# Three layers on one core: the first layer's last six chunks go by seven products in pairs of blocks

## The chip, the cores and the metric

The kernel runs on one core of a Trainium2 chip. The core has five engines with queues of their own: TensorE (PE, matrix products into PSUM, which has eight banks here), VectorE (DVE), ScalarE (ACT), GpSimd (POOL, no access to PSUM) and SyncE (SP, which here only issues DMAs). The metric is the device time of one execution in microseconds (us).

## The reference

Attention with a threshold, and behind it two layers of two products each, on 2304 tokens of width 512:

```python
scores = scale * np.matmul(q, k.transpose(0, 1, 3, 2))          # 4 x 8 heads, 576 x 576, depth 64
thresh = np.max(scores, axis=-1, keepdims=True) - tau
scores = np.where(scores >= thresh, scores, -1000000000.0)
...                                                             # softmax, times v, heads side by side
h = x @ w_in                       # first layer, 512 -> 2048
r = np.maximum(h, 0.0)
g = s * (r * r) + b                # s and b are one number each
x = g @ w_out                      # 2048 -> 512
h = x @ w_in2                      # second layer
g = np.maximum(h, 0.0) + alpha * np.minimum(h, 0.0)
out = g @ w_out2
```

## The kernel before

Everything is float32. A product is made of three matmuls in a faster format: each operand is split into a high and a low part (`mm3`, L512 to L515: low x high, high x low, high x high). So each operand costs a copy on ACT, which makes the high part, and a subtraction on DVE or POOL, which makes the low part. The weights come as 64-bit numbers and are turned into float32 by shifts and masks on DVE (`numbers`).

The program is a list of tasks. Each has an engine or a choice of engines, a duration, buffers and a rank. A planner (`Plan.run`) plays them in time and gives each free engine the ready task of lowest rank; the order that comes out is each engine's order. Two tables, `MOVED_RANKS` and `MOVED_TASKS`, shift single ranks. Transfers have an assumed time in the planner too.

Four stages follow each other on TensorE:

- A: attention, 16 pairs of heads. Transposes bring q and k into place; for the pairs 4 to 15 the split q is copied on by DMA, from `hq` into `q` or `qo`, two copies for each head (L735), before the head's score products (L775) can start. In between, the first layer on the first 1536 tokens, in six blocks of 256, with the first 10 of 16 chunks of 128 columns of w_in. Each chunk passes relu, square, scale and shift (`square`, L548 to L566); the partial sums go to DRAM (`ya`).
- B: the rest of the first layer, in blocks of 384 tokens. The last two blocks take all 16 chunks, the first four blocks the chunks 10 to 15. A chunk is four products of w_in with a quarter of x each (`hidden`), `square_b` (L568 to L586), and four products with w_out.
- C: the second layer's first product. Two blocks are taken together, and a two by two product of quarters is made by seven products and additions (`seven`, and the loop from L1176): operands are sums of quarters, and results come together by ACT copies out of a bank (L1205), DVE additions (L1209) and more matmuls on top of the same bank. 24 such units.
- D: the second layer's second product, also by seven, in nine blocks of 128 rows from each of two blocks. The last additions (L1300, L1304) and stores (L1312) end the program.

Of the kernel before, what the change touches and what calls it, by code (L numbers as in the profile page):

```python
# [17 lines left out]
P = 128  # L18
BIG = 3.0e38
REBIAS = 2.0 ** -112  # L20
NA = 10
# [12 lines left out]
COLD = 5.5  # L34
# [4 lines left out]
BUSY = 180  # L39
# [23 lines left out]
}  # L63
MOVED_TASKS = {
# [74 lines left out]


class Task:
    __slots__ = ("ways", "engine", "fn", "bufs", "needs", "next", "tail", "port")


class Plan:
# [107 lines left out]
def tile_kernel(ctx: ExitStack, tc: tile.TileContext, q, k, v, tau, w1i, w1o, s_in, b_in, w2i, w2o, alpha, out):  # L253
# [732 lines left out]
    with tc.manual_schedule():  # L986
# [24 lines left out]
        for u in range(NA // 2):  # L1011
            u1i[u] = Unit(w1i, "1i", u, W1I[0] + W1I[1] * u, early=True)
# [342 lines left out]
```

## Time and profile before

| | |
|---|---|
| median of 3 runs | 1106.6 us (1106.44 to 1107.65) |
| the profiled execution's own time | 1106.05 us |
| its span, first to last instruction | 1104.2 us |
| granted TensorE clock | 1.00 throughout |
| TensorE busy (matmul) | 1083.9 us, 98% of the span |
| VectorE busy | 912.9 us, 83% |
| ScalarE busy | 762.2 us, 69% |
| GpSimd busy | 347.9 us, 32% |

Busy time is the union of an engine's instructions. Matmuls overlap, so a matmul's own duration (0.33 us for 384 columns) is longer than its share of the engine; the distance from one start to the next is the share. An idle time of an engine is put down to what ended last before it went on.

### The profile page before, as it was taken

The numbers are of one execution on the slowest core, as the hardware profiler recorded it, in microseconds if no ns is written. First come the engines' busy times: TensorE is split into PE (matmuls) and PEld (weight loads), VectorE is DVE, ScalarE is ACT, GpSimd is POOL, SyncE is SP. The second block draws the span as 40 slices with busy tenths as digits, with TensorE's granted clock in tenths as the row PEclk, the third lists the DMA queues.
The fourth block names the chain that finished last, engine by engine and source line by source line (L and its number), as shares of the span: only waits on it lengthen the run. The fifth ranks groups of instructions, "written<-read, shape, count | busy, mean of one in ns | idle before, by whom it ended". The sixth has DMA issues, their size and how long they took to land.

```text
span 1104.2 us, 22123 instructions
## 1 busy us (share of the span) xinstructions
PE 1083.9 (98%) x7552; PEld 1050.5 (95%) x7552; DVE 912.9 (83%) x2043; ACT 762.2 (69%) x1752; POOL 347.9 (32%) x473
## 2 busy tenths in 40 slices
PE   9899999999999999999999999999999999999998
PEld 8677899999999999999999999999999999999998
DVE  5798888888978988666887789889867999999882
ACT  5787877877877877565464467478777987565551
POOL 1576754654736547231000011112100331212111
PEclk9999999999999999999999999999999999999999
DMA  6654454446444553106366554857535475564531
GB/s 125 172 164 130 108 125 129 110 119 156 110 118 99 133 144 81 47 13 202 116 200 191 176 178 150 284 194 236 170 115 165 166 216 163 148 172 131 143 99 39
DMA packets 185265, 158.36 MB, mean 143 GB/s; under 512 B 72000, under 2 KB 162112, under 8 KB 185152
## 3 DMA queue, kind: packets, MB, share of 16 engines
q1 hardware_dynamic: 181424, 154.49, 48.9%
q10 hardware_dynamic: 3728, 2.46, 0.8%
q8 instruction: 59, 0.97, 0.4%
q14 instruction: 54, 0.44, 0.1%
HBM read 91.10 MB, written 44.56 MB: 123 GB/s over the span
## 4 chain that ended last, share of the span: by engine, by line
PE 82%; DVE 7%; ACT 4%; DMA 3%; issue 2%; SPq 1%; POOL 1%; DVEq 0%; ACTq 0%; POOLq 0%
PE bank L513 13%; PE bank L515 13%; PE bank L514 13%; PE bank_b L514 7%; PE bank_b L515 7%; PE bank_b L513 7%; PE sc L775 7%; PE bank L884 7%; PE bank L909 5%; PE bank L913 1%; DMA q<-hq 1%; PE bank L692 1%; DMA qo<-hq 1%; DMA nat<-in_k_dram 1%; DVE wa L491 1%
## 5 line engine op out<-in xcount | busy, mean ns | idle before, releaser
L789 DVE SCALAR_TENSOR_TENSOR e<-sc,mx,e 128x576 f32<-128x576 f32 x144 | 116.1, 812 | 16.7 <-ACT e L787 14.9
L909 PE MATMUL bank<-eyes,e 128*128 128x128 f32 (+1 forms) x640 | 118.7, 274 | 2.5 <-ACT gf L919 1.4
L783 DVE TENSOR_REDUCE mx<-sc 128x1 f32<-128x576 f32 x144 | 107.4, 751 | 14.8 <-PE sc L775 14.1
L513 PE MATMUL bank<-gt,wa 128*128 128x256 f32 (+1 forms) x372 | 116.0, 312 | 0.4 <-ACT rest L551 0.4
L787 ACT ACTIVATE e<-sc,mx 128x576 f32<-128x576 f32 x144 | 106.1, 744 | 13.3 <-DVE mx L783 12.7
L514 PE MATMUL bank<-gt,wa 128*128 128x256 f32 (+1 forms) x372 | 111.8, 301 | 0.1
L515 PE MATMUL bank<-gt,wa 128*128 128x256 f32 (+1 forms) x372 | 111.8, 301 | 0.0
L909 PEld LDWEIGHTS bank<-eyes,e 128*128 128x128 f32 (+1 forms) x640 | 79.7, 139 | 15.2 <-ACT gf L919 2.8
L513 PE MATMUL bank<-xt,wa 128*128 128x256 f32 (+1 forms) x261 | 82.0, 314 | 0.3 <-ACT rest L551 0.3
L785 POOL TENSOR_SCALAR mx<-mx,tau_s 128x1 f32<-128x1 f32 x144 | 47.2, 330 | 94.4 <-DVE mx L783 89.7
L515 PE MATMUL bank<-xt,wa 128*128 128x256 f32 (+1 forms) x261 | 74.7, 286 | 0.0
L514 PE MATMUL bank<-xt,wa 128*128 128x256 f32 (+1 forms) x261 | 74.7, 286 | 0.0
L513 PEld LDWEIGHTS bank<-gt,wa 128*128 128x128 f32 x372 | 70.3, 189 | 1.2 <-ACT rest L551 0.6
L514 PEld LDWEIGHTS bank<-gt,wa 128*128 128x128 f32 x372 | 70.4, 189 | 0.3 <-POOL gt L564 0.3
L515 PEld LDWEIGHTS bank<-gt,wa 128*128 128x128 f32 x372 | 70.3, 189 | 0.0
L775 PE MATMUL sc<-k,q 128*128 128x288 f32 x256 | 61.8, 366 | 2.9 <-DMA q<-hq 1.5
L884 PE MATMUL bank<-gl,vt 128*128 128x256 f32 (+1 forms) x192 | 63.5, 332 | 0.2 <-DVE gl L944 0.2
L884 PE MATMUL bank<-gh,vt 128*128 128x256 f32 (+1 forms) x192 | 57.7, 302 | 0.0
L944 DVE TENSOR_TENSOR gl<-bank,gh 128x256 fp32r<-128x256 f32 (+1 forms) x96 | 43.2, 451 | 15.9 <-ACT gh L942 15.5
L574 ACT ACTIVATE gt<-rest,b_b,s_b 128x384 fp32r<-128x384 f32 x56 | 39.4, 707 | 23.9 <-DVE rest L572 23.2
L954 POOL TENSOR_TENSOR gr<-gf,gh 64x256 fp32r<-64x256 f32 (+1 forms) x48 | 39.4, 822 | 42.1 <-DVE gl L952 37.1
L775 PEld LDWEIGHTS sc<-k,q 128*128 128x128 f32 x256 | 41.5, 190 | 10.4 <-DVE e L789 3.3
(723 smaller groups left out, 4033.9 us busy)
## 6 DMA issues: line engine op xcount, KB each, us to landing
stg<-in_moe_w_in_dram SPq DMA_DIRECT2D x32, 512.0 KB, 4.1
stg<-in_moe_w_out_dram SPq DMA_DIRECT2D x32, 512.0 KB, 4.2
qo<-hq SPq DMA_DIRECT2D x30, 256.0 KB, 4.5
gf<-rest SPq DMA_DIRECT2D x35, 192.0 KB, 1.9
rest<-gf SPq DMA_DIRECT2D x42, 128.0 KB, 3.0
q<-hq SPq DMA_DIRECT2D x18, 256.0 KB, 4.4
xr<-xs SPq DMA_DIRECT2D x6, 768.0 KB, 4.5
yf<-yb SPq DMA_DIRECT2D x24, 192.0 KB, 2.9
```

The costliest lines, as they stand in the source:

```text
L513: nc.tensor.matmul(o, lhsT=wl, rhs=mh, start=first, stop=False, skip_group_check=on_top)
L514: nc.tensor.matmul(o, lhsT=wh, rhs=ml, start=False, stop=False, skip_group_check=on_top)
L515: nc.tensor.matmul(o, lhsT=wh, rhs=mh, start=False, stop=last, skip_group_check=on_top)
L574: t = add("ACT", act(n, 2, True), lambda: nc.scalar.activation(g.t[:, 0, :n], r.t[:, :n], AF.Identity, bias=b_b, scale=s_b), (r,), (g,), r ...
L775: nc.tensor.matmul(sp.t[:, x, :HS], lhsT=o[0][:, c], rhs=o[1][:, x * HS:(x + 1) * HS], start=n == 0, stop=n == len(passes) - 1)
L783: add("DVE", dve(S), lambda sp=sp, mx=mx: nc.vector.tensor_reduce(mx.t[:, 0:1], sp.t[:, :, :HS], op=ALU.max, axis=AX.XY, negate=True), (sp ...
L785: t2 = add("POOL", 0.26, lambda mx=mx: nc.gpsimd.tensor_scalar(mx.t[:, 1:2], mx.t[:, 0:1], -1.0, tau_s, op0=ALU.mult, op1=ALU.subtract), ( ...
L787: add("ACT", act(S, 1), lambda sp=sp, mx=mx, e=e: nc.scalar.activation(halves(e.t), sp.t[:, :, :HS], AF.Exp, bias=mx.t[:, 0:1]), (sp, mx), ...
L789: add("DVE", dve(S) + 0.065, lambda sp=sp, mx=mx, e=e, col=col, sums=sums: nc.vector.scalar_tensor_tensor(halves(e.t), sp.t[:, :, :HS], mx ...
L884: nc.tensor.matmul(o.t[:, :n], lhsT=w.rearrange("p a b -> p (a b)"), rhs=m.t[:, :n], start=c == first and x == 0, stop=c == last and x == ...
L909: nc.tensor.transpose(gt.t[:rows, m:m + P], es[i].t[:, keys], ident)
L944: add("DVE", dve(n), lambda hi=hi, lo=lo, gt=gt: nc.vector.tensor_tensor(lo.t[:, :n], gt.t[:, :n], f32(hi.t[:, :n]), op=ALU.subtract), (gt ...
```

## The change

1. First layer, B. The last two blocks now go through the chunks 0 to 9 alone, as before with `hidden`, and write partial sums to `ya`. After that three pairs of blocks (0,1), (2,3), (4,5) take the chunks 10 to 15 by seven products: three units for each pair, each of two chunks and two blocks. The weights of these six chunks are made into the seven operands once, x into seven operands for each pair and half. The product with w_out stays as it was, chunk by chunk. At the end the partial sums from `ya` are added.
2. Scale and shift leave the chunks. With r the relu, (s r r + b) @ w_out is s (r r @ w_out) + b times the sums of w_out's columns. The sums of columns are built by adding up the w_out tiles (`total`) and four matmuls of one column; ACT applies s and the shift when an output leaves its bank, and one DVE instruction adds s times the partial sum.
3. The second layer's weights are split later: unit 0 from the end of B's first part on, units 1 to 3 in B's last pair, the rest behind B.
4. In the last block of D each of the seven products has a bank of its own.
5. q, k and v are loaded with one DMA for two heads, not one for each. In the first four pairs the two heads' q buffers count apart.
6. The planner's transfer times are new (a start, a time in a common queue, a tail), and both tables of shifts are new, about as long as before.

```diff
 MOVED_RANKS = {
-    10: -53.2, 50: -14.5, 50.1: -0.3, 75: -27.5, 80.1: -30.1, 85: 42.9, 170.1: -6.8, 180: 36.5, 185: 15.7, 195: -32.8, 200: -38.5, 200.1:
...
+    50: -4.5, 50.1: 9.1, 75: -11.4, 95: 37.2, 110: 10.1, 115: 26.1, 140.1: 30.3, 145: -2.5, 150: -9.3, 170: -6.5, 201: 54.1, 205: 16.6, 207:
...
-    def hwdge(fn, reads=(), writes=(), rank=None, kb=128, after=()):
-        return add("SP", 0.6, fn, reads, writes, after, rank, tail=Plan.LAND + kb / 180.0)
...
+    def moved(kb, run):
+        return kb * 64.0 / run * (0.0075 + 0.000051 * run)
...
+    def hwdge(fn, reads=(), writes=(), rank=None, kb=128, run=1536, tail=1.3, after=()):
+        return add("SP", 0.655, fn, reads, writes, after, rank, tail=tail, moved=moved(kb, run))
...
+            if not inner:
+                add([("POOL", pool2(DM), rank), ("DVE", dve(DM), rank + 0.5 * LATER)], 0, lambda e: on(e).tensor_tensor(
+                    total, total, n32.t, op=ALU.add), (n32, of_total), (of_total,), after=(t,), port=True)
...
-            if e == "DVE":
-                nc.vector.scalar_tensor_tensor(x, x, s_b, x, op0=ALU.mult, op1=ALU.mult)
-                nc.vector.tensor_scalar(x, x, b_b, None, op0=ALU.add)
-            else:
-                nc.gpsimd.tensor_tensor(x, x, x, op=ALU.mult)
-                nc.gpsimd.tensor_scalar(x, x, s_b, b_b, op0=ALU.mult, op1=ALU.add)
...
+        add([("POOL", pool2(n), SOON), ("DVE", dve(n), others)], 0, lambda e: on(e).tensor_tensor(
+            r.t[:, :n], r.t[:, :n], r.t[:, :n], op=ALU.mult), (r,), (r,), port=True)
...
-                loads[nm] = [load(nm, 128, lambda e, t=t, src=src, h=h: e.dma_start(
-                    t.t[:, 0:NQ, h, :], src[b, h0 + h, 0:NQ * P, :].rearrange("(p c) d -> p c d", c=NQ)), t) for h in range(2)]
+                loads[nm] = [load(nm, 256, lambda e, t=t, src=src: e.dma_start(
+                    t.t[:, 0:NQ], src[b, h0:h0 + 2, 0:NQ * P, :].rearrange("h (p c) d -> p c h d", c=NQ)), t)]
...
+        def sums_of_columns():
+            for d in range(NC):
+                nc.tensor.matmul(pb.t[:, d:d + 1], lhsT=total[:, d * P:(d + 1) * P], rhs=ones, start=True, stop=True)
...
-        order = sorted(range(len(blocks_b)), key=lambda j: (blocks_b[j][0] < NJA * TA, j))
-        for i, j in enumerate(order):
-            c0, n = blocks_b[j]
-            f0 = NA if c0 < NJA * TA else 0
...
-            stream(range(f0, NF), first, second)
+        pairs = [(0, 1), (2, 3), (4, 5)]
+        for i, j in enumerate(pairs[-1]):
...
+            for f in range(NA + LAG):
...
+        for i, js in enumerate(pairs):
...
+            xq = quarters(xs, lambda b, c, cs=cs: of_xs(cs[b], n), cs, bx_s, xc)
...
+            for c in range(2):
+                ops, sums = seven(xq[c], False, n, bx_s, None, xb_s, None, SOON + 1e-3, ("DVE",), IN_PLACE)
...
+            def product(k, h, start, after, w, xo=xo):
+                def go():
+                    for c in range(2):
+                        mm3(h.t[:, :n], w[k].t[:, 0, c * P:(c + 1) * P], w[k].t[:, 1, c * P:(c + 1) * P],
+                            xo[c][k].t[:, 0], xo[c][k].t[:, 1], start and c == 0, c == 1, True)
...
+            for u in range(NB):
...
+                product(1, ha, True, (), w)
+                p1, t = copy(ha)
...
+                product(2, hb, True, (), w)
+                plus(hb, p1)
+                squared(p1, 0, fa)
+                product(5, hc, True, (), w)
+                p5, t5 = copy(hc)
+                product(6, ha, False, t, w)
+                pu, t = copy(ha)
...
+                    add("ACT", act(n, 2), lambda y=y, t=t, d=d: nc.scalar.activation(
+                        t.t, y.t[:, :n], AF.Identity, bias=shift[:, d:d + 1], scale=s_b), (y, of_shift), (t,), rank=SOON)
...
+                    add("DVE", dve(n) + 0.065, lambda p=p, t=t: nc.vector.scalar_tensor_tensor(
+                        t.t, p.t, s_b, t.t, op0=ALU.mult, op1=ALU.add), (p, t), (t,), x, SOON + 0.5 * (i == len(pairs) - 1), port=True)
...
-                acc = [Buf(moe_s) for _ in range(4)]
+                each = 1 if (i, it) == (len(pairs) - 1, TB // P - 1) else 2
+                acc = [Buf(moe_s) for _ in range(-(-7 // each))]
```

The order of the instructions moves almost everywhere in A. Three places are shown.

SP in A, at the copies from `hq` for two scores, in a row before (`stg` holds x of the first layer, `xs` and `ya` are in DRAM; the score that comes next reads `q_133`):

```order
L731 DMA k_134<-hk_136 64x576 x2
L658 DMA nat_131<-in_v_dram 128x4x64 x2
L526 DMA stg_99<-xs 128x4x256
L1036 DMA ya<-rest 128x2x256
L735 DMA qo_1284<-hq 64x2x512
L735 DMA q_133<-hq 64x2x512 x2
L735 DMA qo_1284<-hq 64x2x512
L665 DMA nat_131<-in_v_dram 64x2x64
```

And SP in A now, at such copies (the score that comes next reads `qo_1275`):

```order
L730 DMA ko_1277<-hk_139 64x576 x2
L730 DMA k_137<-hk_139 64x576
L655 DMA nat_134<-in_v_dram 128x8x64
L662 DMA nat_134<-in_v_dram 64x2x64
L734 DMA qo_1275<-hq 64x2x512 x2
L734 DMA q_136<-hq 64x2x512 x2
L665 DMA nat_134<-in_v_dram 64x2x64
L730 DMA k_137<-hk_139 64x576
```

Before, one copy for the later score stands ahead of the two that are needed first; now the two that are needed first stand together and ahead. The load of v is one DMA of 128x8x64 where it was two of 128x4x64.

TensorE in B before, one chunk's product with w_in (`xb` are the four quarters of x, `wb` a w_in tile, 12 matmuls into one bank):

```order
L513 MATMUL bank_105<-xb_5998,wb_5977 128x384
L514 MATMUL bank_105<-xb_5998,wb_5977 128x384
L515 MATMUL bank_105<-xb_5998,wb_5977 128x384
L513 MATMUL bank_105<-xb_5999,wb_5977 128x384
L514 MATMUL bank_105<-xb_5999,wb_5977 128x384
L515 MATMUL bank_105<-xb_5999,wb_5977 128x384
L513 MATMUL bank_105<-xb_6000,wb_5977 128x384
L514 MATMUL bank_105<-xb_6000,wb_5977 128x384
L515 MATMUL bank_105<-xb_6000,wb_5977 128x384
```

And TensorE in B now, one of the seven products (`bank_111`) between products with w_out (`bank_b_5785`, whose operands lie in `wa`):

```order
L527 MATMUL bank_b_5785<-wa_95,wa_91 128x384
L528 MATMUL bank_b_5785<-wa_95,wa_91 128x384
L529 MATMUL bank_b_5785<-wa_95,wa_91 128x384
L527 MATMUL bank_111<-xb_5776,wb 128x384
L528 MATMUL bank_111<-xb_5776,wb 128x384
L529 MATMUL bank_111<-xb_5776,wb 128x384
L527 MATMUL bank_111<-xt,wb 128x384
L528 MATMUL bank_111<-xt,wb 128x384
L529 MATMUL bank_111<-xt,wb 128x384
```

A product is now six matmuls over two operands of x (there are two halves of the rows), and seven of them stand for what were 16 products of three matmuls, two chunks and two blocks.

TensorE at the program's end before, products 3 and 7 of the last block, both into `bank2`:

```order
L513 MATMUL bank2_107<-gt_104,xt_103 128x256
L514 MATMUL bank2_107<-gt_104,xt_103 128x256
L515 MATMUL bank2_107<-gt_104,xt_103 128x256
L513 MATMUL bank2_107<-wa1_89,wb2_5979 128x256
L514 MATMUL bank2_107<-wa1_89,wb2_5979 128x256
L515 MATMUL bank2_107<-wa1_89,wb2_5979 128x256
```

And now, the same two products:

```order
L527 MATMUL bank0_108<-wa9_100,gt_107 128x256
L528 MATMUL bank0_108<-wa9_100,gt_107 128x256
L529 MATMUL bank0_108<-wa9_100,gt_107 128x256
L527 MATMUL bank1_109<-wa8_99,gt_107 128x256
L528 MATMUL bank1_109<-wa8_99,gt_107 128x256
L529 MATMUL bank1_109<-wa8_99,gt_107 128x256
```

The additions that read product 3 no longer wait for the matmuls of product 7.

## Rows read from the trace of the kernel before

**Rows 1.** The page's head: busy time, share of the span and instructions of each engine.

```profile
span 1104.2 us, 22123 instructions
...
PE 1083.9 (98%) x7552; PEld 1050.5 (95%) x7552; DVE 912.9 (83%) x2043; ACT 762.2 (69%) x1752; POOL 347.9 (32%) x473
```

**Rows 2.** Four stages: span, then busy time (and count) of PE, PEld, DVE, ACT, POOL.

```profile
0.00:505.60 505.60, 492.05 (x3688) 461.58 (x3689) 413.49 (x933) 381.13 (x855) 264.96 (x381) 1.00 0.47 119
505.60:739.00 233.40, 233.34 (x1344) 232.48 (x1343) 191.55 (x382) 138.08 (x264) 21.07 (x22) 1.00 0.57 181
739.00:918.00 179.00, 177.20 (x1018) 175.29 (x1016) 153.84 (x303) 145.21 (x359) 35.21 (x39) 1.00 0.56 182
918.00:1104.20 186.20, 181.36 (x1506) 181.14 (x1506) 154.00 (x428) 97.82 (x276) 26.69 (x31) 1.00 0.45 126
```

**Rows 3.** Starts and durations of 384-column matmuls, eleven in a row.

```profile
739.06 0.33 PE L514 MATMUL bank_b<-xb,wa 128*128 128x384 f32 x1
...
740.79 0.33 PE L515 MATMUL bank<-gt,wb 128*128 128x384 f32 x1
```

**Rows 4.** The critical chain: small fp32 matmuls (two records each), start and duration.

```profile
11.56 1.12 PE bank L860 x10
```

**Rows 5.** TensorE's waits up to 505 us: total, times, longest.

```profile
PE sc L775 <- DMA q<-hq: 3.2, 2, 1.7
...
PE sc L775 <- DMA qo<-hq: 1.3, 2, 1.0
```

**Rows 6.** The critical chain at two of those waits, on either copy.

```profile
263.74 6.05 DMA q<-hq
...
384.86 7.13 DMA q<-hq
```

**Rows 7.** VectorE's groups of instructions: busy, mean ns, idle before.

```profile
L572 DVE TENSOR_TENSOR rest<-bank,rest 128x384 f32<-128x384 f32 x30 | 16.5, 553 | 8.7 <-ACT rest L571 8.5
...
L581 DVE TENSOR_SCALAR rest<-rest,s_b,b_b 128x384 f32<-128x384 f32 x25 | 11.9, 478 | 7.4 <-ACT gt L574 7.3
...
L491 DVE TENSOR_TENSOR wa<-sm,wa 128x256 fp32r<-128x256 f32 x35 | 15.8, 464 | 0.1
...
L1172 DVE SCALAR_TENSOR_TENSOR yb<-yb,nal_b,yat 128x384 f32<-128x384 f32 x2 | 2.2, 1076 | 0.0
...
L1172 DVE SCALAR_TENSOR_TENSOR rest<-rest,nal_b,of 128x384 f32<-128x384 f32 x5 | 3.1, 614 | 0.3 <-ACT of L1171 0.3
```

**Rows 8.** VectorE's groups up to 505 us.

```profile
L556 DVE SCALAR_TENSOR_TENSOR rest<-rest,s_b 128x512 f32<-128x512 f32 x14 | 11.3, 805 | 5.0 <-ACT rest L551 5.0
...
L564 DVE TENSOR_TENSOR gt<-rest,gt 128x512 fp32r<-128x512 f32 x12 | 9.8, 815 | 1.3 <-ACT gt L563 1.2
...
L557 DVE TENSOR_SCALAR rest<-rest,b_b 128x512 f32<-128x512 f32 x14 | 7.7, 551 | 0.5
```

**Rows 9.** Busy time where the second layer's first product ends, as in Rows 2.

```profile
880.00:900.00 20.00, 20.00 (x118) 19.96 (x117) 19.84 (x46) 19.61 (x55) 7.10 (x9) 1.00 0.77 240
900.00:920.00 20.00, 18.28 (x108) 17.35 (x107) 19.47 (x41) 14.85 (x40) 6.88 (x8) 1.00 0.58 182
```

**Rows 10.** TensorE's waits from 739 us on.

```profile
PE bank L513 <- DVE xr L1209: 0.8, 1, 0.8
PE bank_b L513 <- ACT yb L1205: 0.7, 1, 0.7
```

**Rows 11.** The last instructions: start, duration.

```profile
1098.79 0.42 DVE L1300 TENSOR_TENSOR n<-bank,xr 128x256 f32<-128x256 f32 x1 [1.02 <-PE bank L515]
...
1099.13 0.42 DVE L1300 TENSOR_TENSOR rest<-bank,xr 128x256 f32<-128x256 f32 x1
1099.19 0.28 PE L515 MATMUL bank_b<-xb,xt 128*128 128x256 f32 x1
...
1099.79 0.42 DVE L1300 TENSOR_TENSOR yat<-bank_b,rest 128x256 f32<-128x256 f32 x1
...
1100.58 0.71 ACTq L1312 DMA_DIRECT2D out_dram<-rest  x1
```

More of the change, by code (lines that the diff above doesn't have):

```diff
@@ L141 @@
 class Task:
-    __slots__ = ("ways", "engine", "fn", "bufs", "needs", "next", "tail", "port")
+    __slots__ = ("ways", "engine", "fn", "bufs", "needs", "next", "tail", "port", "moved")
 class Plan:
@@ L223, in run @@
                         at(now + us, "free", e)
-                        at(now + us + t.tail, "end", t)
+                        if t.moved:
+                            moving = max(moving, now + Plan.ARRIVE) + t.moved
+                            at(moving + t.tail, "end", t)
+                        else:
+                            at(now + us + t.tail, "end", t)
                         break
@@ L360, in tile_kernel @@
     x_s, xb_s, xr_s = Slots(cut(xt, TA)), Slots(), Slots()
[L361 removed]
+    g_s, gb0_s = Slots(cut(gt, 2 * TA)), Slots()
     def pieces(t):
@@ L401, in mult @@
                 on(e).tensor_scalar(n32.t, f32(word(1)), REBIAS, None, op0=ALU.mult)
-        hwdge(load, (), (raw, *also), rank, 512, after)
+        hwdge(load, (), (raw, *also), rank, 512, 1024 if inner else 4096, 1.3, after)
         add([("DVE", 0.34, rank), ("ACT", act(DM, 0, True), rank)], 0, mult, (raw,), (n32,), port=True)
@@ L711, in scaled @@
                                     nc.scalar.activation(q32[p][:, c], tr.t[:, of], AF.Copy, scale=sc_h[h])
-                            add([("DVE", dve(n) + 0.065, ready), ("ACT", act(n, 1), ready)], 0, scaled, (tr,), (hl,))
+                            x = (add([("DVE", dve(n) + 0.065, ready), ("ACT", act(n, 1), ready)], 0, scaled, (tr,), (qt if tail else qs[h],), x),)
                         continue
@@ L1078, in tile_kernel @@
         of_w = []
-        def stream(fs, first, second):
-            gs = {}
-            for i in range(len(fs) + LAG):
-                if i < len(fs):
-                    gs[fs[i]] = first(fs[i])
-                if i >= LAG:
-                    second(fs[i - LAG], gs.pop(fs[i - LAG]))
-        RB = 2 * LATER
-        full = [last]
-        order = sorted(range(len(blocks_b)), key=lambda j: (blocks_b[j][0] < NJA * TA, j))
-        for i, j in enumerate(order):
-            c0, n = blocks_b[j]
-            f0 = NA if c0 < NJA * TA else 0
+        RB = 2 * LATER
@@ new lines, in tile_kernel, with switch_0, quarters @@
+        add("POOL", 0.01, lambda: bx_s.add(strips(late["xr"][0])), after=chain[0], rank=-2.0)
+        gates = [last]
+        def switch_0():
+            xb_s.add(cut(gt, TB)[:4])
+            t_s.add(strips(rest))
+        add("POOL", 0.01, switch_0, after=last, rank=-2.0)
+        def quarters(src, deps, cs, slots, after):
+            xq = [{}, {}]
+            for b, c0 in enumerate(cs):
+                for c in range(NC):
+                    raw = Buf(slots, "x")
+                    hwdge(lambda raw=raw, c=c, c0=c0: nc.sync.dma_start(raw.t, src[c * P:(c + 1) * P, c0:c0 + n]),
+                          deps(b, c), (raw,), SOON, 192, 1536, 1.4, after)
+                    xq[c % 2][f"{c // 2 + 1}{b + 1}"] = raw, lambda raw=raw: raw.t
+            return xq
@@ L1149, in tile_kernel, with switch_x @@
         RC = 3 * LATER
-        add("POOL", 0.01, lambda: t_s.add(strips(late["xr"][0])), after=chain[0], rank=-2.0)
-        of_1 = set(plan.tasks[:n1] + plan.tasks[n2:]) - set(of_w)
+        of_1 = set(plan.tasks[:n1] + plan.tasks[n2:])
+        k = len(plan.tasks)
+        u2i = [weights("i", u, 250 + u, gates[u] if u < len(gates) else last) for u in range(NF // 2)]
+        k2 = len(plan.tasks)
+        u2o = [weights("o", u, 400 + u, plan.tasks[k:k2]) for u in range(NF // 2)]
+        def switch_x():
+            t_s.add(strips(late["xr"][0]) + strips(late["xw"]))
+        add("POOL", 0.01, switch_x, after=of_x, rank=-2.0)
         def switch_c():
-            t_s.add(strips(rest))
-            xb_s.add(cut(gt, TB))
+            p_s.add([x for t in wa[:8] for x in pieces(flat(t))])
         add("POOL", 0.01, switch_c, after=last, rank=-2.0)
-        add("POOL", 0.01, lambda: t_s.add(late["yb"] + late["yat"]), after=of_1, rank=-2.0)
-        n, seq, xc, late7, late4 = TB, [RC], (), [], []
-        pairs = list(zip(order[::2], order[1::2]))
+        add("POOL", 0.01, lambda: t_s.add(late["yb"] + late["of"] + late["yat"]), after=of_1, rank=-2.0)
+        seq, late7, late4 = [RC], [], []
         g_d = [[Buf() for _ in range(NF // 2)] for _ in pairs]
```

261 lines of the change are left out of this document (178 added, 83 removed), and 38 rows, old and new, of tables (MOVED_RANKS, MOVED_TASKS).

## Prediction

> **What bounds the kernel now.** I read the page's busy times first. TensorE's matmul row is busy for 98% of the span; VectorE follows with 83%, ScalarE with 69%, GpSimd with 32% [rows 1]. A busy share can hide bubbles, so I cut the span where TensorE's work changes [rows 2]: attention with the first layer's first ten chunks (I call it A, to 505.6 us), the rest of the first layer (B, to 739), the second layer's first product (C, to 918), its second product and the end (D). In B TensorE idles 0.06 us in 233.4. In C it idles 1.8 us, in A 13.6, in D 4.8, nearly all of that after its last matmul. So B's length is its count of matmuls and nothing else: 1344 records in 233.4 us are 0.1737 us each, and eleven starts in a row, 739.06 to 740.79, give 0.173 [rows 2, 3]. The granted clock is 1.00, the 2.4 GHz level, in all four stages, so no stage has clock to win back.
>
> Then the waits. In A four waits of TensorE end on the copies that fill q for a score product (q and qo from hq): 3.2 + 1.3 = 4.5 us [rows 5]. In C and D waits are short, and the largest end on VectorE's additions and ScalarE's copies of the seven-product scheme [rows 10].
>
> **The change part by part.**
>
> *Matmuls.* The last six chunks of the first layer are taken for two blocks of 384 columns together. Before, two chunks for two blocks were 2 x 2 x 4 products of three matmuls, 48. Now seven products over two halves of the rows make 7 x 2 x 3 = 42. With three such units in each of three pairs that is 9 x 6 = 54 matmuls of 384 columns fewer, and the order of the program has 54 fewer (2352 before, 2298 now). The product with w_out is unchanged. 54 x 0.173 = 9.3 us, all of it on the path, since B has nothing else in it. New are four fp32 matmuls of one column, which sum w_out's columns. No row shows that shape. The nearest are fp32 matmuls of 128 columns, 0.112 us for each of two records [rows 4]: at most 4 x 0.22 = 0.9 us; at least nothing, if they fall into a gap. They also wait for the last of the sums on VectorE, with B's matmuls queued behind them, so I take 0.6.
>
> *The copies into q.* In A the four waits are those where the order of the program leaves the least between the copy's issue and its reader: 13, 13, 14 and 20 TensorE instructions. In the order of before another DMA stands ahead of or between the two copies that the score needs, at all four places, and at three of them it is a copy for a score that is read later. In the new order all twelve sets stand with the two copies that are read first at the front; the smallest distances are 15, 22, 25, 25 and 27. The copies took 6.05 and 7.13 us at two of the waits [rows 6], so a distance of 22 is no full cover. I count 2.0 us of waiting for the new order against 4.5: 2.5 us less. Bounds: 4.5 less if all of it goes; 3 more if new places are late by as much as the old ones. SP also issues 47 loads of q, k and v where it issued 94, of twice the size; SP isn't late in A on the chain, so I count nothing for that, and it is lost only if the one larger load holds back the first transpose.
>
> *Scale and shift.* They leave every chunk and go to the output. In A 14 pairs of VectorE instructions, 0.805 + 0.551 us, become one multiplication each; on the other hand multiplications and ten column sums move to VectorE, so that it has 27 more plain two-input instructions of 512 columns, near 0.815 us [rows 8]. 27 x 0.815 - 14 x 1.356 = 3 us more; with 7 more conversions at 0.8 and some smaller ones that came forward from B, 13. VectorE is busy 413.5 us of 505.6 in A [rows 2]; 427 is 84%. I cost it at nothing: TensorE's work hides it. If that cover is gone, it costs up to its 13 us (a rival below).
>
> *Vector work in B and C.* By place in the program's order B has 42 more additions and subtractions of 384 columns at 0.553, 19 more scaled additions at 0.614, 25 fewer scalings at 0.478 and 15 fewer 256-wide subtractions at 0.464 [rows 7]: 23.2 + 11.7 - 12.0 - 7.0 = 15.9 us. About ten fewer 512-wide ones take back 5 or so. So VectorE would have 191.6 + 11 = 203 us of B's 233.4 - 9.3 + 0.6 = 224.7, 90%. C has 44 more 256-wide ones and 14 fewer of 384, 20.4 - 7.7, and five more scaled additions: 153.8 + 15.8 = 170 of 179 us, 95%, where it was 86%. This is because the second layer's weights are now split in C, not in B. ScalarE has 75 more instructions of 384 columns in B and stays near 70%. I take 1.0 us for all of it. Bounds: 1 less, if C's 1.8 us of waits shrink, and 6 more (rival 1).
>
> The same scaled addition took 0.614 us in one group and 1.076 in another [rows 7]. The Trainium skill (GPSIMD Engine Reference, Key points) says that GpSimd shares its SBUF interfaces with VectorE and contends with instructions that have two SBUF inputs, as this one has. By that rule a fifth of the added instructions, since GpSimd works 35.2 of C's 179 us [rows 2], would take 0.46 us more: with some 60 of them 5.5 us, VectorE would be full in C, and the sum would carry rival 1's 5.2 where I put 1.0. The trace agrees that one shape takes such different times; that GpSimd is the cause no row here shows.
>
> *The end.* In the last block every one of the seven products gets a bank of its own. Before, products 3 and 7 shared one, so two additions started together when 7 was done, at 1098.79 and 1099.13, and three more followed behind the last matmul to the issue at 1100.58 [rows 11]. Now the addition for product 3 runs under product 7; the chain is one VectorE step shorter, and two from the last matmul. A step is 0.34 us (1098.79 to 1099.13). I take 0.5 us less; between 0 and 0.7.
>
> Sum, on the profiled execution's 1106.05 us: - 9.3 + 0.6 - 2.5 + 1.0 - 0.5 = 1095.35. The median of the runs is 0.55 above it, so I forecast 1095.9 us.
>
> **The rivals.**
>
> 1. *VectorE becomes the bound in C.* In the last 40 us around C's end VectorE is busy 19.84 and 19.47 us of 20, and there TensorE lost 1.72 us [rows 9]. With 95% over all of C the same would come in each of C's three pairs, and in B's last: three times 1.72 more, 5.2. That gives 1101. For it: the counts above. Against it: the order now has the weights of C's first product ready 66 TensorE instructions ahead, where before it was 1, and busy time counts tails that overlap when the engine is full (384-wide additions: 0.55 a piece). That one shape of addition takes from 0.614 to 1.076 us [rows 7] is a reason not to go lower than 0.2.
>
> 2. *Attention gains more.* A's idle time is 13.6 us [rows 2], of which the four waits are 4.5. If the new order removes 9 of it and not 2.5, the time is 1089.4. For it: every instruction of A was ordered anew. Against it: most of these waits are under 1 us and end on engines that are themselves busy. 0.12.
>
> 3. *Slower: VectorE in A.* If VectorE's queue is what paces A, its 13 us more are paid one for one and the saved waits don't come: 1095.9 + 13 + 2.5 = 1111. It decides from the point where VectorE has no idle left beside TensorE's; it has 92 us of it in A now, so this is unlikely: 0.05.
>
> 4. *The seven products don't pay.* Within a unit a product waits for ScalarE's copy of an earlier one out of the same bank, and eight banks also hold the outputs of a block. If each of the nine units loses 1 us, the 9.3 are gone: 1105. Against it: C runs 24 such units and lost 1.8 us in all [rows 2]. 0.06.
>
> **How the numbers follow.** The forecast has 0.57, the rivals 0.2, 0.12, 0.05 and 0.06. The range from 1089 to 1102 takes in rivals 1 and 2 and the bounds of the copies, the small matmuls and the end; it leaves out rivals 3 and 4 and some further tails, under 0.2. A measurement of this kernel can tell about 0.2%, 2.2 us, from no change. Faster by that is everything below 1104.4: the forecast and rivals 1 and 2, with some tail taken off, 0.9; rival 4 falls mostly within 0.2% of before, 0.05; slower 0.05.
>
> **What would show it.** Right: 2298 matmuls of 384 columns at 0.173, B about 225 us and still without idle time, waits on hq's copies below 2.5 us, C within 2 us of 179, the last DMA issued about 1 us after the last matmul starts. Wrong: TensorE waits in B or C that end on VectorE or ScalarE and sum to over 4 us (rival 1 or 4), or A longer than 506 us with VectorE above 90% of it (rival 3).

## The result and the profile after

The changed kernel takes 1096.43 us in the median of six executions (1094.69 to 1098.18), beside 1108.1 for the kernel before in the same series (1106.44 to 1112.17): a ratio of 0.989, with a 95% interval from 0.987 to 0.991. The forecast was 1095.9 us. The profiled execution is the longest of the six, 1098.18 us, so what follows is 1.75 us above the median.

The four stages of the profiled execution after, as in [rows 2]: borders, length, busy time and count of TensorE's matmuls and weight loads, VectorE, ScalarE and GpSimd, granted clock, DMA.

```profile
0.00:502.47 502.47, 492.78 (x3688) 462.20 (x3689) 421.51 (x959) 380.21 (x857) 253.04 (x368) 1.00 0.47 125
502.47:733.30 230.83, 226.55 (x1298) 223.62 (x1297) 196.28 (x390) 143.24 (x314) 20.47 (x21) 1.00 0.55 177
733.30:910.90 177.60, 177.18 (x1018) 175.16 (x1016) 162.74 (x340) 153.74 (x388) 46.71 (x48) 1.00 0.62 203
910.90:1096.40 185.50, 181.30 (x1506) 181.09 (x1506) 151.64 (x420) 99.63 (x271) 25.61 (x33) 1.00 0.45 125
```

Against [rows 2] A is 3.1 us shorter, B 2.6, C 1.4, and D with the end 0.7. B was to give 8.7. In [rows 2] it was busy to 0.06 us; here it stands for 4.3 (230.83 less 226.55). C has VectorE busy for 162.74 of 177.60 us, 92%, and TensorE idle for 0.4.

The waits say where. First those of TensorE in A (total, times, longest), as in [rows 5]; then those in B; then the rest to the end, as in [rows 10].

```profile
PE bank L883 <- ACT gf L918: 3.4, 2, 3.1
PE sc L774 <- DVE e L788: 1.5, 4, 0.5
...
```

```profile
PE bank L527 <- DVE rest L1181: 1.3, 2, 0.7
PE bank_b L527 <- DVE rest L1181: 1.0, 2, 0.7
PE bank L1091 <- DVE total L455: 0.8, 1, 0.8
PE bank L528 <- DVE gt L581: 0.5, 1, 0.5
PE bank_b L528 <- DVE wa L1192: 0.4, 1, 0.4
PE bank L527 <- ACT gt L580: 0.2, 1, 0.2
```

```profile
PE bank_b L527 <- DVE of L1350: 0.3, 1, 0.3
PE bank_b L527 <- ACT rest L1346: 0.2, 1, 0.2
```

In A no wait on a copy from hq is left, where [rows 5] had 4.5 us. One stall is new in size: 3.1 us near 25 us, on gf. ScalarE stands there 5.25 us for the first weight chunk's load, with the copy of gf behind it in its queue. Six other executions with the same order in A show 1.1 to 1.9 there.

In B TensorE waits for L1181, the addition behind product 7. This is how it looks at the end of the first pair: starts and durations of matmuls, and in brackets the idle time and what ended it. The first two are the last of product 7; the next is the first of product 4, which adds into a bank that VectorE must first have read.

```profile
615.71 0.33 PE L528 MATMUL bank<-gt,wb 128*128 128x384 f32 x1
615.88 0.34 PE L529 MATMUL bank<-gt,wb 128*128 128x384 f32 x1
616.87 0.44 PE L527 MATMUL bank<-gt,wb 128*128 128x384 f32 x1 [0.65 <-DVE rest L1181]
617.15 0.34 PE L528 MATMUL bank<-gt,wb 128*128 128x384 f32 x1
```

From start to start that is 0.99 us where [rows 3] have 0.173, so 0.82 is lost, more than the 0.65 in the bracket. All three pairs end so. Counted from start to start beyond 0.173 us, where two starts of 384-column matmuls lie over 0.3 us apart, B loses 6.6 us: 2.5 at the pairs' ends, 1.9 at the column sums, 1.2 in the third pair, 1.1 near 543 us. The column sums (eight records of the four fp32 matmuls, with the wait ahead):

```profile
582.73 0.34 PE L529 MATMUL bank_b<-gt,wa 128*128 128x384 f32 x1
583.86 1.05 PE L1091 MATMUL bank<-ones,total 128*128 128x1 f32 x8 [0.79 <-DVE total L455]
584.77 0.42 PE L527 MATMUL bank_b<-gt,wa 128*128 128x384 f32 x1
```

From 582.73 to 584.77 is 2.04 us, 1.87 more than 0.173. The end of the program, as in [rows 11]: product 3's addition now runs at 1090.87, under product 7. From the last matmul's start to the end of the span it takes 4.4 us, where it was 5.0. But to the last issue it takes 1.35 us, where [rows 11] have 1.39, so the 0.6 us lie behind the last issue. The last addition is done 0.97 us after that start, where it was 1.36; the stores of the result before it, issued at 1092.65, still hold ScalarE's queue for 0.59 us, and the last issue stands behind them.

```profile
1090.87 0.43 DVE L1442 TENSOR_TENSOR xr<-bank,yb 128x256 f32<-128x256 f32 x1 [0.29 <-PE bank L529]
...
1091.99 0.28 PE L529 MATMUL bank<-wb 128*128 128x256 f32 x1
...
1092.54 0.42 DVE L1442 TENSOR_TENSOR rest<-bank,n 128x256 f32<-128x256 f32 x1
...
1092.65 0.59 ACTq L1454 DMA_DIRECT2D out_dram<-of  x1
...
1093.34 0.69 ACTq L1454 DMA_DIRECT2D out_dram<-rest  x1
```

### The profile page after: what moved, and what is told of

Read it like the earlier page. It is cut to its first block, busy times and chain, and to the rows that moved or that the text cites. A ratio compares the mean times of both kernels' runs of the same rounds, so it can differ in the third digit from the quotient of the medians.

```text
span 1096.4 us, 22167 instructions
## 1 busy us (share of the span) xinstructions
PE 1077.8 (98%) x7506; PEld 1042.1 (95%) x7506; DVE 932.2 (85%) x2107; ACT 776.8 (71%) x1829; POOL 345.8 (32%) x469
## 4 chain that ended last, share of the span: by engine, by line
PE 77%; DVE 12%; ACT 3%; issue 3%; DMA 3%; SPq 0%; POOL 0%; DVEq 0%; ACTq 0%; POOLq 0%
PE bank L527 11%; PE bank L528 11%; PE bank L529 11%; PE bank L883 8%; PE sc L774 7%; PE bank_b L527 7%; PE bank_b L528 7%; PE bank_b L529 7%; PE bank L908 5%; PE bank L912 1%; PE bank L690 1%; DMA stg<-in_moe_w_out_dram 1%; DVE n L418 1%; DVE sm L492 1%; PE bank L859 1%
## 5 line engine op out<-in xcount | busy, mean ns | idle before, releaser
L527 PE MATMUL bank<-gt,wa 128*128 128x256 f32 (+1 forms) x291 | 91.8, 315 | 0.2 <-ACT gt L580 0.2
L528 PE MATMUL bank<-gt,wa 128*128 128x256 f32 (+1 forms) x291 | 87.0, 299 | 0.5 <-DVE gt L581 0.5
L529 PE MATMUL bank<-gt,wa 128*128 128x256 f32 (+1 forms) x291 | 86.9, 299 | 0.0
L527 PE MATMUL bank<-xt,wa 128*128 128x256 f32 (+1 forms) x269 | 83.9, 312 | 0.8 <-ACT rest L565 0.7
L784 POOL TENSOR_SCALAR mx<-mx,tau_s 128x1 f32<-128x1 f32 x144 | 50.1, 348 | 89.2 <-DVE mx L782 80.4
L528 PE MATMUL bank<-xt,wa 128*128 128x256 f32 (+1 forms) x269 | 77.5, 288 | 0.0
L529 PE MATMUL bank<-xt,wa 128*128 128x256 f32 (+1 forms) x269 | 77.4, 288 | 0.0
L774 PE MATMUL sc<-k,q 128*128 128x288 f32 x272 | 64.6, 362 | 1.5 <-DVE e L788 1.5
L528 PEld LDWEIGHTS bank<-gt,wa 128*128 128x128 f32 x291 | 55.1, 189 | 1.0 <-DVE gt L581 0.7
L527 PEld LDWEIGHTS bank<-gt,wa 128*128 128x128 f32 x291 | 55.0, 189 | 1.0 <-ACT gt L580 0.5
L529 PEld LDWEIGHTS bank<-gt,wa 128*128 128x128 f32 x291 | 54.9, 189 | 0.0
L527 PEld LDWEIGHTS bank<-xt,wa 128*128 128x128 f32 x269 | 51.0, 190 | 2.4 <-ACT rest L565 1.4
L774 PEld LDWEIGHTS sc<-k,q 128*128 128x128 f32 x272 | 43.9, 191 | 8.6 <-DVE e L788 3.1
```

The costliest lines, as they stand in the source:

```text
L527: nc.tensor.matmul(o, lhsT=wl, rhs=mh, start=first, stop=False, skip_group_check=on_top)
L528: nc.tensor.matmul(o, lhsT=wh, rhs=ml, start=False, stop=False, skip_group_check=on_top)
L529: nc.tensor.matmul(o, lhsT=wh, rhs=mh, start=False, stop=last, skip_group_check=on_top)
L774: nc.tensor.matmul(sp.t[:, x, :HS], lhsT=o[0][:, c], rhs=o[1][:, x * HS:(x + 1) * HS], start=n == 0, stop=n == len(passes) - 1)
L784: t2 = add("POOL", 0.26, lambda mx=mx: nc.gpsimd.tensor_scalar(mx.t[:, 1:2], mx.t[:, 0:1], -1.0, tau_s, op0=ALU.mult, op1=ALU.subtract), ( ...
```

## The experiments

The theory to test: the saved matmuls are worth 9.3 us, B's new waits take back some 5 of them, and A's copies give some 5. The rivals are with each run. Stage lengths given below run from the first matmul of A, B and C to that of the next stage (for C, to its last of 384 columns), found in the same way in each trace; by that count the kernel before has in its profiled execution A 505.6, B 233.8 and C 179.7, and the changed kernel A 502.5, B 231.3 and C 178.2 in its profiled execution, and A 500.5, B 230.2 and C 179.4 in that of `d_end_as_before`, whose order differs only in the last block. The runs come from several series, each with its own executions of the kernel before (medians 1106.7 to 1108.6), so two versions are compared by their ratios to it as well as by their medians; the changed kernel's ratio is 0.989. Where an order is said to be held, it was recorded engine by engine from the planner and given back to it as a list.

**What a matmul is worth in B.**

```diff
-                product(1, ha, True, (), w)
+                product(1, ha, True, (), w, again=2)
```

> The first of the seven products of each of the nine units in B (the rest of the first layer) is issued twice in a row into the same bank, the second time from the start: 9 x 6 = 54 matmuls of 384 columns more, the number that the change saves; nothing else moves and the outputs are those of before. My theory (in B every matmul of 384 columns is on the path at 0.173 us, and the waits of some 5 us that the profile of the changed kernel shows there come on top): 9.3 us more than the changed kernel, 1105.7 where it has 1096.4, B at 239.5 us. Rival (the waits show that VectorE and ScalarE set B's pace, and the saved matmuls were mostly turned into waits): the added matmuls fill the waits, 4 to 6 us more, 1101.

Measured: 1104.96 us (1103.42 to 1106.7), ratio to before 0.9975 (0.9965 to 0.9985). That is 8.5 us above the changed kernel by the medians, 9.4 by the ratios (0.0085 of 1108). B is 238.7 us, 7.4 to 8.5 more, with 4.9 us lost between starts where it was 5.3 to 6.6. The rival expected 1101. So the price of a matmul in B is nearly what the forecast said, and work added at the start of a unit does not fall into the waits: all but 0.4 to 1.7 us of them come on top.

**The pairs' ends.**

```diff
-            second(0, NF - 2)
+            second(0, NA + NB - 1)
             late4.pop()()
...
-            second(0, NA + NB - 1)
+            second(0, NF - 2)
```

> At the end of each of the three pairs in B the changed kernel issues product 4 straight behind product 7, whose bank VectorE must first have read; TensorE stands there three times, about 0.8 us each. Here the product with w_out of a chunk that is long ready (the twelve matmuls of chunk NA + 2 of the pair's first block) comes between them, and that of chunk NF - 2 later. My theory (the wait is the turnaround of one bank and needs only other work to stand in it): the three stalls go, B 2.4 us shorter, 1094.0. Rival (VectorE's queue sets the pace at the pair's end, so that the wait shows up again at the next product that needs it): B within 0.7 us of what it was, 1096.4. The order of C and D comes out otherwise than in the changed kernel in many small places, which can move the total by 2 us either way, so B's length decides.

> The change at the pairs' ends of b_pair_end (twelve matmuls of a chunk that is long ready between products 7 and 4), and the order of all other work held: TensorE's is that of the changed kernel row by row but for these matmuls, the other engines keep theirs as far as the moved matmuls allow. My theory (the three stalls of 0.82 us are the turnaround of a bank, and what b_pair_end lost in the second layer came from its new order there): B 2.5 us shorter than the 230 to 231 of the changed kernel, C and D as in it, 1094.0 in all where the changed kernel has 1096.4. Rival (each us that B gives up comes back in C, because C's split weights and sums are paced by VectorE, which is 91% busy there): B shorter, C longer by as much, 1096.4.

Measured: `b_pair_end` 1099.42 us (1099.07 to 1104.54), slower than the changed kernel by 3 (5.7 by the ratios, 0.9941 to 0.989), with B at 227.3 and C at 186.4. `b_pair_end_rest_kept` 1095.66 us (1094.6 to 1096.37), ratio 0.9886, with B at 228.0 and C at 179.5. In both the three stalls are gone, and B gives 2.2 to 4.0 us, as the theory said. What `b_pair_end` lost is for the most part one wait in C of 4.35 us, for a split weight that the new order brought late, and the slow matmuls behind it: TensorE's matmuls around it, and then the stretch by granted clock (columns as for the stages; the clock is the third number from the end).

```profile
762.08 0.44 PE L527 MATMUL bank<-gt,wa 128*128 128x384 f32 x1 [4.35 <-DVE wa L505]
...
762.76 0.52 PE L527 MATMUL bank<-xb,wa 128*128 128x384 f32 x1
763.08 0.52 PE L528 MATMUL bank<-xb,wa 128*128 128x384 f32 x1
```

```profile
752.00:757.00 5.00, 5.00 (x31) 5.00 (x30) 3.16 (x9) 3.81 (x11) 0.00 (x0) 1.00 0.97 275
...
762.50:765.50 3.00, 3.00 (x12) 3.00 (x11) 2.17 (x6) 1.10 (x3) 0.83 (x2) 0.52 0.74 232
```

After that stop the matmuls start 0.32 us apart, ten of them, at a granted clock of 0.52, nearly all of it the 1.2 GHz level. With the rest of the order kept C is 0.1 to 1.3 us longer than in the two traces of the changed order (179.4 and 178.2), where B is 2.2 to 3.3 us shorter. So the rival, all of it back in C, is wrong, but a part comes back: B and C together take 409.5 and 409.6 us in those two traces, 407.5 here, and 408.2 to 408.4 in the three other runs below that shorten B by 1.8 us or more. The longest waits that are left in B and C of `b_pair_end_rest_kept`:

```profile
PE bank_b L527 <- ACT xr L1346: 1.1, 2, 0.7
PE bank_b L527 <- DVE rest L1181: 0.8, 1, 0.8
PE bank L1091 <- DVE total L455: 0.7, 1, 0.7
```

L1181 has one wait of 0.8 in place of four with 2.3 together. The medians differ by 0.8 us only (0.4 by the ratios), and the executions of either kernel spread over 1.8 to 3.5: that B became shorter is shown, how much of it the total keeps is not.

**The column sums.**

```diff
-        add("PE", 0.9, sums_of_columns, (of_total,), (pb,), rank=SOON)
+        add("PE", 0.9, sums_of_columns, (of_total,), (pb,), rank=2 * LATER + 10.0025)
```

> The four one-column matmuls that sum w_out's columns are issued inside the first unit of seven products in B and not in the stretch ahead of it. My theory (of their cost about 0.8 us is a wait for the last of VectorE's additions into total and the refill of TensorE behind it, 0.7 the four matmuls themselves): B 0.8 us shorter, the wait on total gone. Rival (the cost is that of switching TensorE between kinds of matmul, at any place the same): no change in B. The order behind it comes out otherwise in many small places; B's first 80 us decide.

Measured: 1096.49 us (1095.18 to 1099.8), ratio 0.9911 (0.9882 to 0.994). The wait on total is gone and the loss at the sums fell from 1.8 to 0.8 us, in B 228.4 us. C lost 0.4 to 1.5 us more between starts than in the changed kernel, `b_first_product_twice` and `d_end_as_before`, and the time did not fall. The place in the order set 1 us of their 1.8; the total does not show it.

**The end.**

```diff
-                each = 1 if (i, it) == (len(pairs) - 1, TB // P - 1) else 2
+                each = 2
```

> In the last block the seven products go two to a bank again, as in the kernel before; all else as in the changed kernel. My theory (products 3 and 7 then share a bank, so that two of VectorE's additions wait for 7, one step of 0.34 us more and a second one behind the last matmul): the time from the start of the last matmul to the end of the span goes from 4.4 us to 4.9, 0.5 us more in all. Rival (the end hangs on the last DMA's landing and on ScalarE, and the order of the last additions decides nothing): no change, within 0.2 us.

Measured: 1096.84 us (1095.4 to 1097.28), 0.4 above the changed kernel by the medians and 1.4 by the ratios, less than a measurement can tell from no change. In the trace the time from the last matmul's start to the end of the span is 5.1 us where it was 4.4, and to the last issue 2.20 where it was 1.35. The trace shows the theory's step; the times alone would not.

```profile
1090.09 0.28 PE L529 MATMUL bank<-wb 128*128 128x256 f32 x1
...
1092.29 0.56 ACTq L1454 DMA_DIRECT2D out_dram<-yb  x1
```

**Without the searched tables.** Both tables of moved priorities empty, in either kernel:

```diff
-MOVED_RANKS = {50: -4.5, 50.1: 9.1, ...
-MOVED_TASKS = {25: -0.7, 45: -13.4, ...
+MOVED_RANKS = {}
+MOVED_TASKS = {}
```

> The changed kernel with both tables of moved priorities empty: the planner's rules and costs alone set the order; the work is the same. My theory (the products save 9.3 us against the kernel before whatever the order, and what the tables are worth is waits): slower than the changed kernel by 10 to 25 us, and faster than before_no_table by 8 to 12. Rival (the tables carry the gain, and the change in the work without them is worth nothing): within 3 us of before_no_table.

> The kernel before with both tables of moved priorities empty, for comparison with after_no_table; the work is the same as in the kernel before. My theory: 10 to 25 us slower than the kernel before, 1118 to 1133, and slower than after_no_table by 8 to 12 us. Rival: within 3 us of after_no_table.

Measured: 1111.0 us (1108.68 to 1112.94) and 1120.42 us (1119.64 to 1121.38). The tables are worth 14.6 us in the changed kernel and 12.3 in the kernel before; the rest of the change is worth 9.4 (9.8 by the ratios), the size that the theory gave. But the stages of the two profiled executions, which are 7.0 us apart, show that it isn't where the theory put it. First the changed kernel without tables, then the kernel before without them: A, B, C.

```profile
0.00:510.80 510.80, 497.18 (x3688) 463.50 (x3689) 421.51 (x959) 378.55 (x857) 261.74 (x375) 1.00 0.48 126
510.80:743.95 233.15, 228.05 (x1298) 225.33 (x1297) 199.23 (x389) 148.25 (x320) 25.79 (x24) 0.99 0.57 183
743.95:925.30 181.35, 177.65 (x1017) 174.97 (x1016) 160.42 (x331) 152.04 (x386) 44.05 (x47) 1.00 0.55 182
```

```profile
0.00:520.76 520.76, 498.88 (x3688) 461.47 (x3689) 422.15 (x955) 379.75 (x848) 265.18 (x386) 1.00 0.46 119
520.76:753.70 232.94, 232.86 (x1344) 232.54 (x1343) 181.40 (x364) 130.54 (x256) 19.87 (x22) 1.00 0.51 159
753.70:931.60 177.90, 176.94 (x1017) 175.10 (x1016) 161.41 (x325) 147.99 (x364) 37.27 (x38) 1.00 0.63 206
```

B is the same in both, 233: the units of seven products, ordered by the rules alone, lose in waits (and 1.5 us of slow clock) all that their 54 matmuls save. C is 3.4 us longer and D 0.7 shorter. A is 10.0 us shorter. There TensorE's waits for ScalarE's relu of a hidden chunk were 7.3 us without the change (first line) and 2.4 with it (second). Which part of the change in A does that (no scale and shift, larger loads, the planner's new transfer times) was not separated.

```profile
PE bank L487 <- ACT rest L525: 7.3, 10, 2.0
...
PE bank L509 <- ACT rest L547: 2.4, 4, 0.8
```

**The copies into q.** The kernel before, its order held row by row, but SP's order at the four places of [rows 5]:

```diff
 SP near 262 us:
 q<-hq
-stg<-xs
 q<-hq
 qo<-hq x2
+stg<-xs
```

> The kernel before, its whole order held row by row, but for the four sets of copies from hq into q at which TensorE waited in stage A (0.29, 1.51, 1.02 and 1.67 us at 157, 270, 298 and 392 us): there SP issues the two copies that the next score product reads one behind the other, ahead of the set's other two and of the load or copy that stood between. My theory (these waits are the lateness of those copies, and the order of SP's issues makes them late): of the 4.5 us 2.6 go, by the time that the second copy is issued earlier at each place (0.3 of 0.3, 0.6 of 1.5, 1.0 of 1.0, 0.7 of 1.7), so A ends at 503.0 in place of 505.6, and the time is 2.6 us under that of the kernel before. Rival (another wait behind takes their place, and A's gain in the changed kernel comes from the scale and shift that left it): under 1 us.

Measured: 1102.94 us (1101.91 to 1103.67), ratio to before 0.9953 (0.9941 to 0.9965): 5.2 us less, between 3.9 and 6.5. In the trace A is 502.0 us where it was 505.6, no wait on hq is left, and the last matmul starts 4.1 us earlier. The theory's mechanism holds and its size was too small: all of the 4.5 us of waits went, not 2.6, and with some others a little longer A is 3.7 us shorter. Why more went than the earlier issue explains is open. SP's issues at the second of the places, beside which no wait stands any more:

```profile
262.61 1.32 SPq L735 DMA_DIRECT2D q<-hq  x2
263.98 2.23 SPq L735 DMA_DIRECT2D qo<-hq  x2
266.25 0.61 SPq L526 DMA_DIRECT2D stg<-xs  x1
```

A run that was to show the reverse in the changed kernel went wrong:

> The changed kernel, but in ten of its sets of four copies into q (attention, stage A) SP issues the two copies that are read last ahead of the two that are read first; nothing else moves. My theory (A's gain of some 5 us comes from the four waits on such copies, and these went because the two that are read first stand at the front, with little to spare): waits of TensorE on copies from hq come back, 2 to 5 us in all, and the time goes to 1099 to 1101. Rival (the places in the order are so far ahead that the copies' order does not matter, and the waits went through the distance alone): none comes back, 1096.4.

Its edit swapped the copies from hk into k and not those from hq into q, so it says nothing on q. It took 1097.07 us (1095.28 to 1098.4), with no wait on a copy from hk: those have room for two issues. That the order of q's copies decides is shown by the run above alone.

**Work added on VectorE and GpSimd.**

```diff
-            r.t[:, :n], r.t[:, :n], r.t[:, :n], op=ALU.mult), (r,), (r,), port=True)
+            ..., on(e).tensor_scalar(r.t[:, :n], r.t[:, :n], 1.0, None, op0=ALU.mult)], (r,), (r,), port=True)
...
-            t = add(ways(("DVE", "POOL")), 0, lambda e, a=a, o=o: on(e).tensor_tensor(
+            t = add(ways(("DVE", "POOL")), 0, lambda e, a=a, o=o, m=1 + (left and rank >= 250 and rank < 400 and k in (1, 2, 6)): [on(e).tensor_tensor(
```

> The changed kernel's order, with work added in place. In A each of the 30 squarings is followed by a multiplication by one on the same engine, where the kernel before scaled and shifted: 18 on VectorE, some 0.55 us each, 10 in all (421 to 431 us of A's 501), and 12 on GpSimd, some 0.77 each. In C 18 of VectorE's subtractions of 256 columns, for the split weights, are issued twice, 0.46 each, 8 us in all (163 to 171 us of C's 178, 96%). My theory (TensorE's work hides it in A, and in C VectorE has slack as long as it is under the span): A and C within 1 us of the changed kernel's (500.5 and 179.4), 1097 in all. Rival for A (part of A's gain is the shorter way from a hidden row to its square): A 2 us or more longer. Rival for C (at over 95% VectorE sets the pace): C 5 us or more longer.

Measured: 1119.45 us (1117.08 to 1121.16), 23 more than the changed kernel. Both halves of my theory fell. (11 of the 18 subtractions ran within C, where VectorE's busy time rose by 6.7 us.) A is 515.9 us, 15 more than the 500.5 to 501.3 of the same order without the work, though VectorE is busy only 429 us of it. C is 185.2, 6 more, with VectorE at 169.5 of 184.6:

```profile
0.00:515.93 515.93, 500.91 (x3688) 464.45 (x3689) 428.97 (x977) 381.89 (x857) 271.29 (x380) 1.00 0.46 122
...
747.50:932.05 184.55, 178.89 (x1018) 174.95 (x1016) 169.49 (x353) 154.94 (x389) 45.42 (x48) 1.00 0.60 197
```

GpSimd's multiplications took 1.53 us each, 18.4 in all, and VectorE's 8.5 in all. VectorE's waits for mx, which GpSimd scales ahead of each of the 144 exponentials, went from 0.5 to 4.6 us. How the 15 us divide between the two engines was not separated. Here an order that was fitted to one set of work had no slack for another, whatever the busy shares say; whether C's 6 us come from that or from a VectorE that is full was not separated. The run does not show what the scale and shift cost in the kernel before, whose order was fitted to them.

**A better version.** Two more orders of the changed kernel. The edit at the start is this, on ScalarE:

```diff
-n<-stg (L410)
 gf<-bank (L918)
 sh<-bank (L918)
 e<-sc,mx (L786)
+n<-stg (L410)
```

> The changed kernel with three edits of its order, the rest held as far as these allow: the pairs' ends as in b_pair_end_rest_kept, the column sums inside the first unit as in b_sums_later, and near 21 us ScalarE's first conversion of a weight chunk (and VectorE's step behind it) a few places later, since ScalarE stands 3.8 us there for the chunk's load with copies in its queue for which TensorE waits 1.7 us, and 0.5 for a copy behind. My theory (each is a stall by the order alone, with nothing behind it): A 2.2 us shorter, B 3.4, 1090.8 in all. Rival (the waits move on to the next place, as half of them did in b_pair_end_rest_kept): 1094 to 1096.

> b_pair_end_rest_kept with one more edit: ScalarE's first conversion of a weight chunk (at 24.7 us of the trace, 3.8 us behind the instruction ahead of it) stands three places later, behind the copies of gf and sh and the exponentials that are ready at 22 to 24 us, and VectorE's two steps on the same chunk behind its next scaled sum. In three_edits the planner put that conversion back in its old place, as the trace shows, so that edit has not been run yet. The rest is in the order of b_pair_end_rest_kept, row by row. My theory (a stall of the order alone): TensorE's waits of 1.7 and 0.5 us near 25 and 28 us go, B begins at 498.6 in place of 500.8, and the time is 2.2 us under b_pair_end_rest_kept's 1095.7: 1093.5. Rival (the same load is what the following weight steps wait for, and the wait moves to them): 0.5 us or less.

Measured: `three_edits` 1096.53 us (1095.8 to 1098.8), ratio 0.99, no gain. Its third edit never took place, as ScalarE's line shows (the first fence: the conversion still stands ahead of the copy of gf), and ahead of the first unit TensorE waited 0.5 us for ScalarE's copy at L580 instead. `pair_end_and_start` 1094.35 us (1094.07 to 1095.56), ratio to before 0.9883 (0.9865 to 0.9901). There the stall on gf went, and most of it came back 1.5 us long at the next product that needs ScalarE (second fence, waits of TensorE in A). A is 1.4 us shorter than in `b_pair_end_rest_kept`, C 1.1 longer, and the time is 1.3 us less by the medians but 0.3 by the ratios: nearer to the rival than to the theory.

```profile
24.72 0.66 ACT L410 ACTIVATE n<-stg 128x512 f32<-128x512 f32 x1 [3.81 <-DMA stg<-in_moe_w_in_dram]
25.29 0.36 ACT L918 ACTIVATE gf<-bank 128x256 f32<-128x256 f32 x1
```

```profile
PE bank L690 <- ACT q L710: 1.5, 1, 1.5
...
PE bank L883 <- ACT gf L918: 0.2, 1, 0.2
```

Its median is the lowest measured, 2.1 us under the changed kernel's, but by the ratios it is 0.8 us, so that it is faster is not shown.

## Why the prediction was right, and where only its sum was

The time came out within 0.5 us of the forecast, by errors that cancel; that it came so near is luck.

- *Matmuls, - 9.3.* The count and the cadence are right (2298 at 0.173), and 54 of them are worth 8.5 to 9.4 us when put back. But the term was taken as B's whole change, since "B has nothing else in it". That was true before and is no longer: B lost 6.6 us between starts, and gave 2.5 to 3.6 us and not 8.7. This is the step that failed. By the prediction's own sign (waits in B and C on VectorE or ScalarE above 4 us; they are 4.7) the forecast's case was wrong there, and rival 4's mechanism, priced at 1 us for each of nine units and put on ScalarE's copies, was half right: 0.82 us at three of them, on VectorE's addition, since in a pair's last unit nothing stands between products 7 and 4. That could have been read from the planned order, in which product 4 follows product 7 directly at these three places.
- *Column sums, + 0.6.* 1.87 us in the profiled execution, three times the term, 1.0 of which the place in the order set. The bound of 0.9 left out the wait ahead, 0.8, that the text named.
- *Copies into q, - 2.5.* All 4.5 us of waits went, the bound of that term. The kernel before with just these issues in order gains 3.9 to 6.5 us: this part alone is a third to a half of the change's 11.7. In the profiled execution the new stall near 25 us, with slow matmuls behind it, hides 1.2 to 2.0 of it.
- *Scale and shift in A, 0.* VectorE's busy time rose by 8 us, not 13, and A did not pay. The reason given, that TensorE's work hides it, does not hold as it stands: 8.5 us on VectorE and 18.4 on GpSimd in unchanged order cost 15. That it was hidden because the order had been made anew around it is likely but not shown: without tables the changed kernel's A is shorter too.
- *Vector work in B and C, + 1.0.* VectorE's busy time rose by 4.7 us in B and 8.9 in C, where the counts gave 11 and 15.8. C has VectorE at 92% and is 0.3 to 1.4 us shorter, so rival 1 did not come. It may have been near: with VectorE's busy time raised from 163 to 169.5 in a held order C took 6 us more, about rival 1's 5.2.
- *GpSimd's share.* By the rule of the Trainium skill (GPSIMD Engine Reference, Key points), that GpSimd contends with instructions of VectorE that have two SBUF inputs, the sum would have made 1100. The traces agree with the rule, but not with that price. In C of the kernel before, 71 scaled additions of 384 columns had no GpSimd instruction beside them and took 0.61 us each, none over 0.63; the 23 that had one took 0.86 on average. In the changed kernel GpSimd worked 47 us of C, more than the 35 before, and 62 of these additions took 0.61 us and 37 took 0.70. So the cost in these additions fell from 5.8 to 3.2 us. One such pair in the kernel before, and the next addition without GpSimd beside it:

```profile
768.05 0.74 POOL L491 TENSOR_TENSOR wb<-stg,wb 128x256 fp32r<-128x256 f32 x1 [14.66 <-ACT wb L490]
768.15 1.05 DVE L1172 SCALAR_TENSOR_TENSOR yb<-yb,nal_b,yat 128x384 f32<-128x384 f32 x1
...
769.83 0.62 DVE L1172 SCALAR_TENSOR_TENSOR yat<-yat,nal_b,yb 128x384 f32<-128x384 f32 x1
```

- *The end, - 0.5.* 0.6 less from the last matmul to the end of the span, and 0.7 back with the old banks. The size is right, but against the kernel before it lies behind the last issue, which came 1.35 us after the last matmul's start and not the 1 us of the prediction's sign. Why the time behind the issue fell, from 3.6 to 3.1 us, is open.

Rival 2, more from A than the copies, has some truth: in the executions without the 3.1-us stall A is 4.3 to 5.2 us shorter.

So of the 7.0 us between the profiled executions without tables A gives 10.0 and C takes 3.4 back, and with tables, of 7.9 us, 3.1 come from A, 2.6 from B, 1.4 from C and 0.7 from the end. What the search was worth to B is shown too: 233 us without it, 230 to 231 with it.

## What to carry to other kernels

Fewer matmuls in a stage that TensorE fills pay only as far as the new dependences leave TensorE other work: look in the new order, place by place, at what stands between two products that share a bank, before the saving is counted. Read the waits that end on a DMA first, and ask in what order their queue issues; here four changed places in a queue were worth a third to a half of what the whole change gave. A busy share of 85% does not mean that 15% more work is free once the order has been fitted.

## What the runs showed of the hardware

A stop of TensorE of 4.35 us in the second layer (`b_pair_end`) was followed by a granted clock of 0.52 over the 3 us from 762.5 on, and the 3.1-us stall near 25 us in the changed kernel by clocks of 0.72 (26.7 to 30 us) and 0.81 (30 to 34). In `d_end_as_before` the stop of 1.7 us near 25 us and the 1.75 us at the column sums left the mean clock at 1.00; where the column sums waited 1.5 us and took 2.8 in all, in the changed kernel without tables, ten matmuls shortly behind them started 0.32 us apart:

```profile
591.00:594.50 3.50, 1.97 (x15) 1.65 (x14) 3.13 (x8) 1.46 (x4) 0.01 (x1) 1.00 0.33 115
594.50:597.50 3.00, 3.00 (x11) 3.00 (x10) 3.00 (x6) 0.47 (x2) 0.00 (x0) 0.50 0.00 0
```

GpSimd took 1.53 us for a multiplication of 128 x 512 by a constant, in place (first fence, the run with added work), and 0.774 for the scale and shift of the same shape by two columns of scalars (second fence, the kernel before). Why is open.

```profile
L568 POOL TENSOR_SCALAR rest<-rest 128x512 f32<-128x512 f32 x12 | 18.4, 1534 | 1.1
```

```profile
L560 POOL TENSOR_SCALAR rest<-rest,s_b,b_b 128x512 f32<-128x512 f32 x16 | 12.4, 774 | 1.8
```
